# Reordering the first loads of a fused sketched-attention and GELU kernel on one Trainium2 core

## The chip, the cores and the metric

The kernel runs on one core of one Trainium2 chip. The core has five instruction streams: TensorE (PE in the profile; its weight loads are listed apart as PEld), VectorE (DVE), ScalarE (ACT), GpSimd (POOL) and SyncE (SP), which here only issues transfers. Transfers between the chip's memory and the core's on-chip buffer are issued by SyncE and, for a few, by ScalarE; sixteen DMA engines carry them out. The metric is the device time of one execution in microseconds. Before the change it is 258.27 us, the median of three runs (258.11 to 258.56).

## What is computed

Attention with polynomial sketches, for 4 batches, 4 heads, 1088 tokens and 32 channels per head, and behind it a feed-forward layer with an exact GELU:

```python
def phi(x):
    a = np.einsum('rd,bhsd->bhsr', S1, x)     # r = 8
    b = np.einsum('rd,bhsd->bhsr', S2, x)
    return np.einsum('bhsi,bhsj->bhsij', a, b).reshape(*x.shape[:-1], r * r)
q_p, k_p = phi(q), phi(k)
kv = np.einsum('bhsf,bhsd->bhfd', k_p, v)
z = np.sum(k_p, axis=2)
attn = einsum('bhsf,bhfd->bhsd', q_p, kv) / (einsum('bhsf,bhf->bhs', q_p, z)[..., None] + 1e-06)
x = attn.transpose(0, 2, 1, 3).reshape(4352, 128)
h = x @ w_in                                   # w_in: 128 x 2048
out = (0.5 * h * (1 + erf(h / sqrt(2)))) @ w_out   # w_out: 2048 x 128
```

`q`, `k` and `v` are float32. `S1`, `S2`, `w_in` and `w_out` arrive as float64; the kernel rounds them to float32 itself, with integer and float instructions on their two 32-bit words.

## The kernel before

Each batch's 1088 tokens are split into 1024 main tokens, in two chunks of 512, and a remainder of 64. The feed-forward layer runs over eight main chunks and one last chunk of all remainders. For each chunk sixteen slices of 128 hidden channels are computed (L740), put through the GELU on ScalarE (L747) and projected back (L826 and L925); between these, in a list of slots by step, the attention of the following chunks is worked out. This part begins at about 15 us and reaches to the end. Every engine's instructions keep the order of the program's text: dependencies at its end tie each instruction to the one before it on the same engine.

Ahead of it lies the start, which the change touches. It does batch 0's attention in its own way, and gets the first weights ready.

Loads. `S1` and `S2` go to one small tile, `raw_SR`. Batch 0's keys are loaded in two halves, heads 0 and 2, and heads 1 and 3 (`load_main`, L103); the queries of batch 0 in two halves by heads, each with both chunks (`load_first_q`, L120); the values by heads as the keys; the remainders' keys of batches 0 and 2 and the values of batch 0 (`load_rem`, L136). Then the first piece of `w_in` follows (`load_w_in(0)`, L181). The second piece is gated: GpSimd writes one word of its tile (L180), so that the transfer is not issued before GpSimd has come to that point. `load_rest` then issues all other weights and the other batches.

Work. TensorE first multiplies zeros into a bank that nobody reads (`keep_busy`, L957). VectorE rounds the sketches (class `Rounding`): exponent fields (L283), the scaled exponent and its clamp (L275 and L277), the low words (L278), the mantissa fields (L288), the mantissas (L302), the signs (L307), and the product, written once for each head, `SR_heads` (L317). The same class can put the low words (L270) and the clamped exponents (L294) on ScalarE, as it does for the weights. `sketches` turns `SR_heads` on TensorE (L334); VectorE makes from it `S12` (L335), the stationary sketches of the four heads, and `sT` (L337), from which GpSimd makes `Srep` (L340). `key_turn` transposes the keys of heads 0 and 2 on TensorE (L348), copied to `kT` by ScalarE (L350); `key_turn_apart` does heads 1 and 3, in two banks (L376), copied by ScalarE and VectorE (L378). `query_turn(0)` transposes chunk 0's queries on VectorE (L551). `key_features` multiplies `kT` with `S12` (L397) and forms the outer products `k_p` (L408 to L412). `expand_products` does the same for queries (L570), `expand_copy` copies (A_sb, L576), `expand_multiply` multiplies (q_pT, L581). `kv_first` sums `k_p` with the values (L445), which GpSimd and ScalarE have widened by a column of ones (L360). The remainder follows (L348, L421, L430, L451). `kz_apart` is the copied sum (L1000), `numerators_by_token` multiplies it with the queries' features (L685), `divide` divides (L696 to L700), and the turned quotient is the feed-forward layer's input `xT`. Between these VectorE, ScalarE and GpSimd round the first two pieces of `w_in` and of `w_out` (L283 to L312).

Of the kernel before, what the change touches and what calls it, by code (L numbers as in the profile page):

```python
# [16 lines left out]
def kernel(  # L17
# [18 lines left out]
    pe, dve, act, pool, sp = nc.tensor, nc.vector, nc.scalar, nc.gpsimd, nc.sync  # L36
    B, H, S, D = q.shape
    R = S1.shape[0]
# [4 lines left out]
    NP = H // 2  # L43
    J = S // 128
    MAIN = J * 128
    REM = S - MAIN
    JC = 4
# [20 lines left out]
    def work_banks():  # L68

        return wps.tile([128, 2, CW], FP, name="w_ps")  # L70

    def work_bank():
        return work_banks()[:, 0]
# [4 lines left out]
    def hidden_bank():  # L78
        return hps.tile([128, CW], FP, name="h_ps")

    def out_bank():
        return ops.tile([128, CW], FP, name="o_ps")


    by_act, by_dve, by_pool = act.copy, dve.tensor_copy, pool.tensor_copy
# [8 lines left out]
    q_first = big.tile([128, H, J, D], FP, name="q_first")  # L94
# [7 lines left out]
    def load_main(eng, n, b, heads=slice(0, H)):  # L102
        eng.dma_start(out=main[n, b][:, heads],  # L103
                      in_=src_of[n][b, heads, 0:MAIN, :].rearrange("h (p j) d -> p h j d", j=J))
# [10 lines left out]
        for g in range(4):  # L115
            sp.dma_start(out=main["v", b][g * 32:(g + 1) * 32].rearrange("t h n d -> t h (n d)"), in_=src[g])

    def load_first_q(c):
        heads = slice(2 * c, 2 * c + 2)
        sp.dma_start(out=q_first[:, heads], in_=q[0, heads, 0:MAIN, :].rearrange("h (p j) d -> p h j d", j=J))  # L120

    def load_q(n):
        at = n % NCH * CW
# [11 lines left out]
    def load_rem(n, b):  # L135
        sp.dma_start(out=rem[n][b // 2 * REM:(b // 2 + 1) * REM, b % 2],  # L136
                     in_=src_of[n][b, :, MAIN:S, :].rearrange("h p d -> p h d"))
# [13 lines left out]
    def landing(dst, wide):  # L151

        if wide:
            rows, n = dst.shape
            if n == 512:

                if not half_block:
                    half_block.append(block())
                    r = half_block[0][:, 0:2]
                else:  # L160
                    r = half_block.pop()[:, 2:4]
                raw[dst.name] = r.rearrange("p a b -> p (a b)").rearrange("p (n two) -> p n two", two=2)
            elif n == 256:
                raw[dst.name] = small(U32).rearrange("p (n two) -> p n two", two=2)
            else:
                raw[dst.name] = big.tile([rows, n, 2], U32, name=f"raw_{dst.name}")
            return raw[dst.name].rearrange("p n two -> p (n two)")
        return dst

    def words(a):  # L170

        return (a, 1) if a.dtype == FP else (a.bitcast(U32), 2)

    def load_w_in(i, gated=False):
        src, e = words(moe_w_in)
        c0, c1 = pieces[i]
        to = landing(w_in_sb[i], e == 2)
        if gated:

            pool.memset(to[0:1, 0:1], 0)  # L180
        sp.dma_start(out=to, in_=src[:, c0 * e:c1 * e])  # L181
# [10 lines left out]

    S_dst = landing(SR, S1.dtype != FP)

    for i, (queue, s) in enumerate(((act, S1), (sp, S2))):
        s, e = words(s)
        queue.dma_start(out=S_dst[i * R:(i + 1) * R, :], in_=s)
    for r, queue in enumerate((sp, act)):
        load_main(queue, "k", 0, slice(r, H, 2))
    nc.scalar.preload_act_table_set("gelu_and_others")  # L200
    for c in range(NP):
        load_first_q(c)
    load_main(sp, "v", 0, slice(0, H, 2))
    for b in (0, 2):
        load_rem("k", b)
    load_main(sp, "v", 0, slice(1, H, 2))
    load_rem("v", 0)
    load_w_in(0)

    def load_rest():  # L210
# [121 lines left out]
    def sketches():  # L332
        ps = work_bank()
        pe.transpose(ps[:, :2 * R], in_=SR_heads.rearrange("r h d -> r (h d)"), identity=ident[:2 * R, :2 * R])  # L334
        dve.tensor_mul(out=S12, in0=ps[:, None, :2 * R].broadcast_to([128, H, 2 * R]),  # L335
                       in1=mask4[:, :, None].broadcast_to([128, H, 2 * R]))
        dve.tensor_copy(out=sT, in_=ps[:, :2 * R])  # L337
        for i in range(2):
            src = sT[:, 0:R, None] if i == 0 else sT[:, None, R:2 * R]
            pool.tensor_copy(out=Srep[:, i], in_=src.broadcast_to([128, R, R]))  # L340
# [12 lines left out]
    def four_tokens(n, b, h, c):  # L353
        return main[n, b][:, h, c * JC:(c + 1) * JC, :].rearrange("p j d -> p (j d)")
# [13 lines left out]
    def key_turn(b, r, ps, copy, midway=lambda: None):  # L368
        kT[r] = transposed(ps, "kT", [four_tokens("k", b, h, c) for h in (r, r + 2) for c in range(NCH)], copy, midway)

    def key_turn_apart(b, r, banks, copies):

        kT[r] = att.tile([128, CW], FP, name="kT")
        for h, ps in zip((r, r + 2), banks):
            for c in range(NCH):
                pe.transpose(ps[:, c * 128:(c + 1) * 128], in_=four_tokens("k", b, h, c), identity=ident)  # L376
        for i, (ps, copy) in enumerate(zip(banks, copies)):
            copy(out=kT[r][:, i * 256:(i + 1) * 256], in_=ps[:, :256])  # L378
# [161 lines left out]
    def query_turn(n, copy=by_act):  # L540


        if n == 1:
            turned = transposed(hidden_bank(), "qT", [q_sb[1][:, h].rearrange("p j d -> p (j d)") for h in range(H)], copy)
            qT[n] = turned.rearrange("p (h j t) -> p h j t", h=H, j=JC)
            return
        qT[n] = att.tile([128, H, width[n] // 128, D], FP, name="qT" if n < NMAIN else "qT_rem")
        if n == 0:
            for c in range(NP):
                heads = slice(2 * c, 2 * c + 2)  # L550
                dve.transpose(out=qT[n][:, heads].rearrange("p h j t -> p h (j t)"),  # L551
                              in_=q_sb[n][:, heads].rearrange("p h j d -> p h (j d)"))
            return
        dve.transpose(out=qT[n].rearrange("p h j t -> p (h j t)"),
                      in_=q_sb[n].rearrange("p h j d -> p (h j d)") if n < NMAIN else q_rem.rearrange("p s b n d -> p (s b n d)"))
# [398 lines left out]
    def keep_busy(n, ps, cols=256):  # L954
        for i in range(n):
            noughts = [nc.const_aps.tensor(0.0, [128, m], FP) for m in (128, cols)]
            pe.matmul(ps[:, CW - cols:], lhsT=noughts[0], rhs=noughts[1], start=True, stop=True)  # L957

    bank = work_bank()
    keep_busy(2, bank, 448)  # L960
    r = Rounding(SR)
    r.fields(by_dve=True)
    r.mantissas()
    r.signs()
    r.product_for_heads(SR_heads)
    sketches()
    key_turn(0, 0, hidden_bank(), by_act)
    key_turn_apart(0, 1, [hidden_bank(), work_bank()], (by_act, by_dve))
    query_turn(0)
    widen_v(0)  # L970
    banks = [out_bank(), out_bank()]
# [185 lines left out]
    for n in range(3, NCHUNK):  # L1157

        t = (n - 1) * NF
        b = (n + 1) // 2 if n % 2 else n // 2  # L1160
# [41 lines left out]
    for t, (n, fi) in enumerate(steps):  # L1202
# [19 lines left out]
        elif fi % NB == NB - 1:  # L1222
            b = fi // NB
# [11 lines left out]
    for t in range(len(steps) + LAG):  # L1235
        if t < 4:
# [14 lines left out]
            if t == 3:  # L1251
                banks = work_banks()
# [23 lines left out]
        if t < len(steps):  # L1276
            n, fi = steps[t]
            hidden(n, fi, by_halves=t >= 18)
        if t < len(steps) and steps[t][0] < NMAIN and steps[t][1] % NB == NB - 1:
            n, b = steps[t][0], steps[t][1] // NB  # L1280
# [50 lines left out]
```

## Time and profile before

| | |
|---|---|
| median of three runs | 258.27 us |
| profiled execution | 257.91 us, of which the span from first to last instruction is 256.1 |
| stages of the span (us) | PE busy, DVE busy, ACT busy |
| 0 to 3.91 | 3.14, 1.75, 1.28 |
| 3.91 to 5.51 | 1.40, 0.42, 0.64 |
| 5.51 to 9.18 | 3.67, 3.02, 2.03 |
| 9.18 to 14.89 | 5.71, 5.42, 4.49 |
| 14.89 to 22.49 | 7.60, 6.89, 4.82 |
| 22.49 to 256.10 | 230.43, 138.51, 101.20 |

A line of the timeline gives the start in the span and the duration in us, the engine, the line of the kernel, the operation, what it writes and reads, the shapes, how often, and in brackets how long the engine was idle before it and what ended that. Times of several merged instructions run from the first one's start to the last one's end. SPq and ACTq are the streams that issue transfers; the time to landing counts from the start of the issue to the end of the transfer. The ends of matmuls are modelled, so PE counts as busy in some short waits too; the starts are the safer guide.

### The profile page before, as it was taken

To read this page: it belongs to the slowest core of one execution; us is meant where nothing else is said; L and a number is where in the kernel's file an instruction comes from. 1 tells how busy PE (TensorE), PEld (TensorE's weight loads), DVE (VectorE), ACT (ScalarE), POOL (GpSimd) and SP (SyncE) were. 2 spreads that over 40 slices of the span, in tenths; PEclk is the share of its full clock that TensorE was granted. 3 is DMA by queue.
4 is the path that set the end of the run, shared out by engine and by line. 5 is a ranking of instruction groups with operands and counts; after the bars stand their busy time and mean duration, and the time that the engine had idled before them with its cause. 6 is when DMAs were issued, how large, how long until landed. Compare 5 with 4: busy or idle time off the path is not lost.

```text
span 256.1 us, 5952 instructions
## 1 busy us (share of the span) xinstructions
PE 251.9 (98%) x2407; PEld 131.5 (51%) x2407; DVE 156.0 (61%) x330; ACT 114.5 (45%) x221; POOL 171.7 (67%) x191
## 2 busy tenths in 40 slices
PE   8999999999999999999999999999999999999994
PEld 4755444255454545454444455455544444445784
DVE  4896889969698987580278976399307000700382
ACT  3784766523535333533335332623444334433541
POOL 3413008799969777587758774787758777877950
PEclk9999999999999999999999999999999999999999
DMA  6789548610001101101000001000200200020021
GB/s 209 217 280 292 153 122 205 204 26 12 0 3 17 25 4 23 21 13 31 0 3 0 0 15 31 1 4 0 38 6 7 37 0 4 5 36 3 0 36 31
DMA packets 29083, 13.50 MB, mean 53 GB/s; under 512 B 21888, under 2 KB 27264, under 8 KB 29056
## 3 DMA queue, kind: packets, MB, share of 16 engines
q1 hardware_dynamic: 28624, 12.79, 20.1%
q8 instruction: 19, 0.31, 0.5%
q10 hardware_dynamic: 432, 0.33, 0.4%
q14 instruction: 8, 0.07, 0.1%
HBM read 10.88 MB, written 2.23 MB: 51 GB/s over the span
## 4 chain that ended last, share of the span: by engine, by line
PE 98%; ACT 0%; DVE 0%; issue 0%
PE h_ps L740 45%; PE o_ps L826 33%; PE o_ps L925 5%; PE w_ps L896 2%; PE w_ps L456 1%; PE w_ps L604 1%; PE w_ps L659 1%; PE w_ps L957 1%; PE w_ps L570 1%; PE o_ps L922 1%; PE h_ps L756 1%; PE o_ps L445 1%; PE w_ps L1043 1%; PE h_ps L348 1%; PE w_ps L685 0%; PE o_ps L397 0%
## 5 line engine op out<-in xcount | busy, mean ns | idle before, releaser
L740 PE MATMUL h_ps<-xT,w_in 128*64 128x512 f32 (+2 forms) x536 | 137.1, 568 | 0.0
L747 ACT ACTIVATE block<-h_ps 128x512 f32<-128x512 f32 (+1 forms) x128 | 73.0, 571 | 116.3 <-PE h_ps L740 114.4
L826 PE MATMUL o_ps<-block,w_out 128*64 128x256 f32 x224 | 57.5, 379 | 0.0
L740 PEld LDWEIGHTS h_ps<-xT,w_in 128*64 128x64 f32 (+1 forms) x536 | 40.7, 140 | 30.3 <-issue 11.6
L791 POOL TENSOR_TENSOR bits_low<-block 128x512 f32<-128x512 f32 x28 | 36.3, 1296 | 27.4 <-ACT block L747 27.4
L826 PEld LDWEIGHTS o_ps<-block,w_out 128*64 128x64 f32 x224 | 30.5, 137 | 38.0 <-issue 27.5
L792 POOL TENSOR_TENSOR bits_a<-block 128x512 f32<-128x512 f32 x28 | 35.7, 1276 | 11.7 <-ACT block L747 11.6
L841 DVE COPY sums<-o_ps 64x256 f32<-64x256 f32 x8 | 3.3, 417 | 60.6 <-PE o_ps L826 60.6
L793 POOL TENSOR_TENSOR bits_e<-bits_a,block 128x512 f32<-128x512 f32 x28 | 36.0, 1287 | 2.2
L794 POOL TENSOR_TENSOR bits_m<-block,bits_e 128x512 f32<-128x512 f32 x28 | 35.8, 1277 | 2.2
L826 PE MATMUL o_ps<-block,small 128*64 128x256 f32 x112 | 28.8, 379 | 0.0
L826 PE MATMUL o_ps<-bits_low,small 128*64 128x256 f32 x112 | 28.8, 379 | 0.0
L826 PE MATMUL o_ps<-bits_a,small 128*64 128x256 f32 x112 | 28.8, 379 | 0.0
L826 PE MATMUL o_ps<-bits_m,w_out 128*64 128x256 f32 x112 | 28.7, 379 | 0.0
L826 PEld LDWEIGHTS o_ps<-block,small 128*64 128x64 f32 x112 | 15.2, 137 | 17.9 <-issue 10.8
L826 PE MATMUL o_ps<-bits_e,small 128*64 128x256 f32 x112 | 17.1, 383 | 0.0
L925 PE MATMUL o_ps<-g,w_out 128*128 128x512 f32 (+1 forms) x34 | 16.5, 572 | 0.0
L826 PEld LDWEIGHTS o_ps<-bits_m,w_out 128*64 128x64 f32 x112 | 15.3, 137 | 0.0
L616 DVE STREAM_TRANSPOSE w_ps<-w_ps 128x512 f32<-128x512 f32 (+1 forms) x7 | 4.8, 687 | 17.1 <-ACT xT L670 12.7
L826 PEld LDWEIGHTS o_ps<-bits_a,small 128*64 128x64 f32 x112 | 15.2, 137 | 0.0
L826 PEld LDWEIGHTS o_ps<-bits_low,small 128*64 128x64 f32 x112 | 15.2, 137 | 0.0
L826 PEld LDWEIGHTS o_ps<-bits_e,small 128*64 128x64 f32 x112 | 7.7, 137 | 10.6 <-issue 8.8
(223 smaller groups left out, 318.5 us busy)
## 6 DMA issues: line engine op xcount, KB each, us to landing
block<-in_moe_w_in_dram SPq DMA_DIRECT2D x3, 512.0 KB, 9.8
block<-in_moe_w_out_dram SPq DMA_DIRECT2D x3, 512.0 KB, 12.0
k<-in_k_dram SPq DMA_DIRECT2D x12, 128.0 KB, 2.7
v<-in_v_dram SPq DMA_DIRECT2D x12, 128.0 KB, 3.6
q<-in_q_dram SPq DMA_DIRECT2D x24, 64.0 KB, 2.4
out_dram<-oT SPq DMA_DIRECT2D x21, 64.0 KB, 2.2
q_first<-in_q_dram SPq DMA_DIRECT2D x2, 256.0 KB, 3.8
v<-in_v_dram SPq DMA_DIRECT2D x2, 256.0 KB, 4.1
```

What stands on the lines that cost most here:

```text
L348: pe.transpose(ps[:, i * 128:(i + 1) * 128], in_=s, identity=ident)
L616: dve.transpose(out=tok, in_=ps[:, :, :H2])
L740: pe.matmul(ps[rows, :W], lhsT=w[:, rows], rhs=xT[n][:, :W], start=True, stop=True)
L747: act.activation(out=g_of[n, fi][:, :W], in_=ps[:, :W], func=ACT.Gelu)
L791: pool.tensor_sub(out=s[3], in0=a11, in1=a21)
L792: pool.tensor_add(out=s[1], in0=a21, in1=a22)
L793: pool.tensor_sub(out=s[2], in0=s[1], in1=a11)
L794: pool.tensor_sub(out=s[4], in0=a12, in1=s[2])
L826: pe.matmul(acc[n][bank][half * 64:(half + 1) * 64, col:col + HW], lhsT=fixed, rhs=moving, start=opens and e == 0 and name in "4715", stop ...
L841: dve.tensor_copy(out=N[lo, 0, one], in_=a0[lo, one])
L896: pe.matmul(acc[NMAIN][rows, COLS_REM[name]], lhsT=tokens[:, rows], rhs=fixed, start=k == 0 and name == ORDER_REM[0], stop=k == BLOCKED // ...
L925: pe.matmul(o_of[n][:, cols], lhsT=w_tile(w_out_sb, fi), rhs=g[:, cols], start=first, stop=final)
```

## The change

The issues of the first loads get another order and other queues, the sketches are rounded in part on ScalarE, their turn moves behind part of the keys' turns, and the idle multiplications get narrower.

- Both sketches are issued on ScalarE's queue, and both halves of the keys on SyncE's, as its first issues.
- The queries of batch 0 are loaded by chunks, all four heads each, not by heads. In memory a run of them is then 4 tokens of 32 channels (512 bytes) and not 8 (1 KB). Chunk 0 follows the keys; then come both halves of the values, the remainders, chunk 1, and the first piece of `w_in`.
- The two idle matmuls cover 344 columns and not 448.
- The sketches' low words and clamped exponents are made by ScalarE (L270 and L294), not VectorE (L275 to L278).
- `sketches` is called inside `key_turn_apart`, between the transposes of head 1 and of head 3.

```diff
-    def load_first_q(c):
-        heads = slice(2 * c, 2 * c + 2)
-        sp.dma_start(out=q_first[:, heads], in_=q[0, heads, 0:MAIN, :].rearrange("h (p j) d -> p h j d", j=J))
+    def load_first_q(n):
+        tokens = slice(n * JC, (n + 1) * JC)
+        sp.dma_start(out=q_first[:, :, tokens], in_=q[0, :, 0:MAIN, :].rearrange("h (p j) d -> p h j d", j=J)[:, :, tokens])
...
-    for i, (queue, s) in enumerate(((act, S1), (sp, S2))):
+    for i, s in enumerate((S1, S2)):
         s, e = words(s)
-        queue.dma_start(out=S_dst[i * R:(i + 1) * R, :], in_=s)
-    for r, queue in enumerate((sp, act)):
-        load_main(queue, "k", 0, slice(r, H, 2))
+        act.dma_start(out=S_dst[i * R:(i + 1) * R, :], in_=s)
+    for r in range(2):
+        load_main(sp, "k", 0, slice(r, H, 2))
     nc.scalar.preload_act_table_set("gelu_and_others")
-    for c in range(NP):
-        load_first_q(c)
-    load_main(sp, "v", 0, slice(0, H, 2))
+    load_first_q(0)
+    for r in range(2):
+        load_main(sp, "v", 0, slice(r, H, 2))
     for b in (0, 2):
         load_rem("k", b)
-    load_main(sp, "v", 0, slice(1, H, 2))
     load_rem("v", 0)
+    load_first_q(1)
     load_w_in(0)
...
-    def key_turn_apart(b, r, banks, copies):
+    def key_turn_apart(b, r, banks, copies, midway=lambda: None):

         kT[r] = att.tile([128, CW], FP, name="kT")
         for h, ps in zip((r, r + 2), banks):
+            if h == r + 2:
+                midway()
             for c in range(NCH):
                 pe.transpose(ps[:, c * 128:(c + 1) * 128], in_=four_tokens("k", b, h, c), identity=ident)
...
-    keep_busy(2, bank, 448)
+    keep_busy(2, bank, 344)
     r = Rounding(SR)
-    r.fields(by_dve=True)
+    r.low_words()
+    r.fields()
+    r.exponents()
     r.mantissas()
     r.signs()
     r.product_for_heads(SR_heads)
-    sketches()
     key_turn(0, 0, hidden_bank(), by_act)
-    key_turn_apart(0, 1, [hidden_bank(), work_bank()], (by_act, by_dve))
+    key_turn_apart(0, 1, [hidden_bank(), work_bank()], (by_act, by_dve), sketches)
     query_turn(0)
```

## The prediction

> **What bounds the kernel now.** I read the page first: busy shares and the chain that ended last.
>
> ```profile
> span 256.1 us, 5952 instructions
> PE 251.9 (98%) x2407; PEld 131.5 (51%) x2407; DVE 156.0 (61%) x330; ACT 114.5 (45%) x221; POOL 171.7 (67%) x191
> PE 98%; ACT 0%; DVE 0%; issue 0%
> ```
>
> TensorE is the chain, so the question is where it waits or works on nothing. The stages' busy times answer: from 22.49 to the end PE is busy 230.43 of 233.61 us, and no list of waits from there names a load that holds it up. Whatever the first 22 us gain or lose moves the rest of the program with it, one for one. So I read the start as a timeline:
>
> ```profile
> 3.14 0.86 PE L957 MATMUL w_ps<-const-float32-0.0 128*128 128x448 f32 x1
> 3.62 0.28 DVE L317 TENSOR_TENSOR SR_heads<-bits_m,bits_e 16x128 f32<-16x128 f32 x1
> 4.05 0.20 PE L334 MATMUL w_ps<-ident,SR_heads 16*128 16x16 f32 x1
> 4.18 0.66 PE L348 MATMUL h_ps<-ident,k 128*128 128x128 f32 x4
> 4.36 0.22 DVE L335 TENSOR_TENSOR S<-w_ps,mask 128x64 f32<-128x64 f32 x1 [0.46 <-PE w_ps L334]
> 4.70 0.44 PE L376 MATMUL h_ps<-ident,k 128*128 128x128 f32 x2
> 4.87 0.58 ACT L350 COPY kT<-h_ps 128x512 f32<-128x512 f32 x1 [1.77 <-PE h_ps L348]
> 5.39 0.42 DVE L378 COPY kT<-w_ps 128x256 f32<-128x256 f32 x1 [0.73 <-PE w_ps L376]
> 5.51 0.69 PE L397 MATMUL o_ps<-S,kT 128*64 128x64 f32 x16 [0.16 <-ACT kT L350]
> 5.73 0.80 DVE L551 STREAM_TRANSPOSE qT<-q_first 128x256 f32<-128x256 f32 x2
> ```
>
> The reader is to see a relay: idle columns to 4.00, the sketches' turn, the turns of the keys, ScalarE's copy, and only at 5.51 the first useful product. S12 (L335) was ready at 4.58; the copy of kT (4.87 to 5.45) came last.
>
> Then the loads, in the list of DMA issues (last column: us to landing) and VectorE's waits:
>
> ```profile
> q_first<-in_q_dram SPq DMA_DIRECT2D x2, 256.0 KB, 3.8
> k<-in_k_dram SPq DMA_DIRECT2D x1, 256.0 KB, 2.8
> k<-in_k_dram ACTq DMA_DIRECT2D x1, 256.0 KB, 3.3
> small<-in_moe_w_in_dram SPq DMA_DIRECT2D x1, 256.0 KB, 3.2
> DVE bits_e L283 <- DMA small<-in_moe_w_in_dram: 0.5, 1, 0.5
> ```
>
> With their issues (1.19 and 1.37 for the keys, 1.66 and 2.15 for the queries, 2.68 for the first values, 5.96 for the first w_in) they land at 3.97, 4.67, 5.36, 6.05, 6.78 and 9.16. 256 KB every 0.70 us: a full pipe, in which w_in is last, and VectorE waits 0.53 us for it. From 9.18 to 14 VectorE is busy 95% (5.42 of 5.71 us to 14.89), and it feeds what PE waits for there. So two arms matter: keys to products (PE, ScalarE), and the arrival of w_in (VectorE).
>
> **The change, part by part.**
>
> *Loads.* The first keys' issue moves from 1.19 to SyncE's first place, 0.73. They landed 2.78 us after issue: 3.51. The rest follows at the pipe's pace: second keys 4.21 (4.67 before). They leave ScalarE's queue and the second sketch takes their place there, so both issues of that queue still end at 1.79, and its table load still runs 1.82 to 3.10. SyncE loses one issue (0.40) and gains one (0.42).
> The queries now come as runs of 512 bytes, 512 of them per load, not 256 of 1 KB. The trace has 256 runs of 1 KB at 0.70, and 256 of 128 bytes (each remainder) at 0.28: from first values (6.78) to remainder values (8.32) are 1.54, less 0.70 for the second values, over three. Linear in runs and bytes this gives 0.92 for the new form; the low end is 0.70, as before. I take 0.80, between them, since the runs lie nearer to 1 KB than to 128 bytes in what they carry. [...]
> So chunk 0's queries land at 5.01, values at 5.71 and 6.41, three remainders at 7.25, chunk 1's queries at 8.05, w_in 0.84 later (its step before) at 8.89, against 9.16: 0.27 earlier, between 0.03 (0.92 each) and 0.47 (0.70 each). SyncE is not the limit: five issues of 0.42 to 0.49 and three of 0.60 to 0.76 bring w_in's issue to 5.9 as before, and an issue on an empty pipe (the second w_in, 8.5) took 2.8.
> Chunk 1's queries, moved past both values and three remainders, are read at 10.12 by L348: 2 us of cover. Values and remainders only come earlier. GpSimd's widening of v waits for values (6.83 before) and starts at 5.7, then waits for ScalarE's a_t; its memset that gates the second w_in moves from 8.42 to about 7.7. That buys nothing: that w_in, landed by 11.3, is first read at 12.08.
>
> *Sketches.* The second one is issued at 1.37 and not 0.73; the pair landed 1.57 after issue, so 2.94, at worst with the first keys whose packets it shares the engines with, 3.51. I take 3.05, nearer the small load. VectorE loses three instructions (0.17, 0.17, 0.16). ScalarE gains two; the nearest row is a_rem, 128x64, 0.21. They lie in its 1.77 us of idleness. The first can't start before the table load ends at 3.10. Chain: e 0.39 (3.44), r on ScalarE 0.21 plus handover (3.75), signs to SR_heads 0.48 as before (3.42 to 3.90): 4.23, 0.33 later than now.
>
> *PE's order.* Idle columns: four records, 0.75 from start to start, scaled by 344/448 to 0.58: they end at 3.26 and not 4.00. The keys' turns then wait for the landing at 3.51, start at 3.55 and end 0.66 later, 4.21. ScalarE copies from 4.24 to 4.82. Behind them two turns for head 1 (landed 4.21; 4.25 to 4.53), the sketches' turn at 4.53 (SR_heads has been there for 0.3), S12 from 4.84 to 5.06, and first products at 5.12 against 5.51: 0.39 gained. Two turns of head 3 and its copy sit behind the sketches' turn on PE: head 3 turned by 5.0, VectorE's copy after S12 and sT, at 5.12 against 5.39, second products 5.6 against 6.03. VectorE then runs its packed row (qT, k_p) 0.27 earlier, and chunk 0's queries (5.01) are there in time for qT at 5.46.
>
> *Sum.* The PE and ScalarE arm gains 0.39 up to A_sb and kz_apart (8.86 and 10.24 now); the VectorE arm gains 0.27 at w_in, where it would otherwise wait. The smaller one decides, since both meet at the numerators' division (11.49): 0.27 us. The profiled execution took 257.91 (256.1 of span and 1.81 around it), 0.36 below the median of three, 258.27; the sum gives 257.64 on its scale, **258.00** on the median's.
>
> **Rivals.**
>
> *PE is still slow when the keys come (slower).* The loads of the weights show two speeds of the array: 335 ns for 128 columns among the idle columns, 138 ns in the keys' turns.
>
> ```profile
> L957 PEld LDWEIGHTS w_ps<-const-float32-0.0 x4: 285/335/337, 0.7 to 2.4; 128*128 128x128 f32 x4
> L348 PEld LDWEIGHTS h_ps<-ident,k x4: 138/140/142, 4.2 to 4.5; 128*128 128x128 f32 x4
> ```
>
> The switch lay after 2.4 and before 4.02, with PE at work since 0.77. Now the columns end at 3.26 and PE pauses a quarter of a microsecond; turns that begin at 3.55 may still run slowly, 0.2 us more each. Three slow ones eat the gain (copy of kT to 5.42). With all up to the sketches' turn slow (3.55 plus six by 0.335 is 5.56, 0.51 for the turn itself, 0.28 for S12) products start at 6.35, 0.84 late: 259.1. With the 32 products slow too (16 loads take 0.55, so 34 ns more each, 1.1 us) 260.2. It decides if the speed comes later than about 4.5, and costs over 0.52 from about 5.5.
> For it: idle columns exist only to fill this time. Against it: the switch in the trace may lie well before 3.5; the last idle record is 0.10 shorter than the middle ones (857 to 954 ns).
> [...]
>
> *Nothing is gained.* The queries' 512-byte runs cost 0.92 each, w_in lands at 9.13, and all that PE wins is spent waiting there: 258.2.
>
> *More is gained.* Full rate for the queries, w_in at 8.69, and VectorE's first instruction on it, which took 0.64 after the wait (0.28 to 0.41 elsewhere), finds data nearly there. With PE's arm at its 0.39 and this 0.2 more: 257.6 to 257.75.
>
> **How the numbers follow.** 0.2% is 0.52 us, about what a measurement of this kernel tells from no change. Forecast (gain of 0.1 to 0.55): 0.46, of which 0.06 lies beyond 0.52. More gained: 0.14, at its far end beyond it too. Nothing gained: 0.13. Slow PE: 0.27, all slower. Faster 0.20, same 0.53, slower 0.27. The forecast's own range is 257.75 to 258.2; 257.5 to 259.1 takes in both gains and the nearer half of the slow case, leaving out some 0.17.
>
> **What would show it.** Right: first keys' turn near 3.55 with loads at 138 ns, first products near 5.1, w_in landing near 8.9, VectorE still waiting for it a few tenths, and the stage from 22 us on unchanged in length and shifted by 0.3. Wrong: loads of 280 ns or more behind 3.5; SR_heads after 4.5, with PE idle before L334; queries landing over 0.9 after the keys; or a new wait of the division (11.49) on something not named here.

## The result, and the profile after

The changed kernel takes 259.02 us in the median (22 executions, 258.22 to 260.15), the kernel before beside it 258.28 (22 executions, 257.94 to 258.81): a ratio of 1.0033, 95% interval 1.0019 to 1.0046. It is slower by about 0.85 us by the ratio, and by 0.74 between the medians, where 0.27 us of gain was forecast.

The two ranges say as much as the medians. Sorted, the changed kernel's times fall into two groups: twelve from 258.22 to 259.10, none in between, ten from 259.61 to 260.15. The kernel before has one group only. Even the first group's median, 258.67, lies 0.4 above that of the kernel before. The profile was taken of an execution of the first group (258.30, span 256.5), so it shows only one part of the story; a profile of the second group comes with the experiments.

First the page of the changed kernel (span, busy shares, chain by engine), which has changed little:

```profile
span 256.5 us, 5953 instructions
PE 252.2 (98%) x2407; PEld 132.2 (52%) x2407; DVE 155.7 (61%) x327; ACT 115.1 (45%) x223; POOL 172.2 (67%) x191
PE 97%; DMA 1%; ACT 0%; DVE 0%; issue 0%
```

Then its timeline (start, duration, engine, line, what, and in brackets the idle time before it and what ended that); lines behind the insertion of the diff have moved by two, so L399 is the old L397:

```profile
0.77 2.63 PE L959 MATMUL w_ps<-const-float32-0.0 128*128 128x344 f32 x4 [0.77 <-PEq L1318]
3.55 0.71 PEld L348 LDWEIGHTS h_ps<-ident,k 128*128 128x128 f32 x4 [1.16 <-POOL v_rem_aug L245]
3.64 0.17 DVE L283 TENSOR_SCALAR bits_e<-raw_SR 16x32 uint32<-16x32 uint32 x1 [2.54 <-DMA raw_SR<-in_S_dram]
4.25 0.43 PEld L378 LDWEIGHTS h_ps<-ident,k 128*128 128x128 f32 x2
4.47 0.28 DVE L317 TENSOR_TENSOR SR_heads<-bits_m,bits_e 16x128 f32<-16x128 f32 x1
4.71 0.58 ACT L350 COPY kT<-h_ps 128x512 f32<-128x512 f32 x1 [0.48 <-PE h_ps L348]
4.86 0.14 PEld L334 LDWEIGHTS w_ps<-ident,SR_heads 16*128 16x128 f32 x1 [0.17 <-DVE SR_heads L317]
5.20 0.23 DVE L335 TENSOR_TENSOR S<-w_ps,mask 128x64 f32<-128x64 f32 x1 [0.45 <-PE w_ps L334]
5.54 0.58 PEld L399 LDWEIGHTS o_ps<-S,kT 128*64 128x64 f32 x16 [0.32 <-ACT kT L350]
6.04 0.77 DVE L553 STREAM_TRANSPOSE qT<-q_first 128x256 f32<-128x256 f32 x2
9.29 0.29 DVE L283 TENSOR_SCALAR bits_e<-small 128x256 uint32<-128x256 uint32 x1 [0.41 <-DMA small<-in_moe_w_in_dram]
```

The keys do come earlier, and their turns start at 3.55 and not 4.18. But the four weight loads of the first turns take 0.71 us, not 0.42, and the two of head 1 take 0.43, not 0.20: the array is at its lower rate until between 4.46 and 4.86. The slow turns start 0.21 us apart (3.82, 4.03, 4.25, 4.46), those of the kernel before 0.11 (4.35, 4.46, 4.56): about half the rate. The sketches are read at 3.64 and not 2.30; the PE waits 0.17 us for `SR_heads`. The first products start at 5.54, where they started at 5.51 before. The head start of 0.63 us is used up within 2 us, even in this quick execution. The first `w_in` (issued at 6.14, 3.1 to landing) is read at 9.29, 0.11 later than before.

### The profile page after: what moved, and what is told of

Read it like the earlier page. It is cut to its first block, busy times and chain, and to the rows that moved or that the text cites. A ratio compares the mean times of both kernels' runs of the same rounds, so it can differ in the third digit from the quotient of the medians.

```text
span 256.5 us, 5953 instructions
## 1 busy us (share of the span) xinstructions
PE 252.2 (98%) x2407; PEld 132.2 (52%) x2407; DVE 155.7 (61%) x327; ACT 115.1 (45%) x223; POOL 172.2 (67%) x191
## 4 chain that ended last, share of the span: by engine, by line
PE 97%; DMA 1%; ACT 0%; DVE 0%; issue 0%
PE h_ps L742 45%; PE o_ps L828 33%; PE o_ps L927 5%; PE w_ps L898 2%; PE w_ps L458 1%; PE w_ps L606 1%; PE w_ps L661 1%; DMA k<-in_k_dram 1%; PE w_ps L572 1%; PE o_ps L924 1%; PE h_ps L348 1%; PE h_ps L758 1%; PE o_ps L447 1%; PE w_ps L1046 1%; PE w_ps L687 0%; PE o_ps L399 0%
## 5 line engine op out<-in xcount | busy, mean ns | idle before, releaser
L742 PE MATMUL h_ps<-xT,w_in 128*64 128x512 f32 (+2 forms) x536 | 137.1, 568 | 0.0
L742 PEld LDWEIGHTS h_ps<-xT,w_in 128*64 128x64 f32 (+1 forms) x536 | 40.7, 140 | 30.3 <-issue 11.6
```

Source lines behind the costliest of these rows:

```text
L742: pe.matmul(ps[rows, :W], lhsT=w[:, rows], rhs=xT[n][:, :W], start=True, stop=True)
```

## The experiments

Two reasons compete for the loss, with a third that the forecast had leant on. *Clock theory*: the narrower idle columns leave the PE without work before the keys have landed, and the array then gets its full rate late. *Sketch theory*: the second sketch, behind the keys' issue, delays `S12`. *Load theory*: the queries' 512-byte runs and the new order delay the queries and `w_in`. Each set of runs had executions of the kernel before beside it on the same chip. In the table "late" counts executions at 259.6 us and above.

| kernel | median us (lowest to highest) | late | ratio to before, 95% interval |
|---|---|---|---|
| before, in four sets | 258.36, 258.50, 258.41, 258.63 (257.92 to 258.93) | 0 of 34, 35, 29, 17 | |
| changed, again | 259.34 (258.16 to 261.93) | 6 of 12 | 1.0040 [1.0015, 1.0066] |
| changed, 448 columns | 258.65 (258.16 to 260.86) | 1 of 12 | 1.0012 [0.9994, 1.0030] |
| changed, 512 columns | 259.05 (258.22 to 260.98) | 1 of 12 | 1.0025 [1.0008, 1.0042] |
| changed, second sketch on SyncE first | 259.91 (258.56 to 261.08) | 7 of 12 | 1.0053 [1.0034, 1.0073] |
| changed, the same and 448 columns | 258.66 (258.45 to 259.28) | 0 of 11 | 1.0010 [1.0001, 1.0019] |
| before, 344 columns | 259.47 (258.94 to 260.35) | 5 of 11 | 1.0047 [1.0032, 1.0061] |
| before, 400 columns | 258.59 (257.99 to 260.45) | 5 of 12 | 1.0030 [1.0006, 1.0054] |
| before, 512 columns | 258.62 (257.97 to 259.06) | 0 of 12 | 1.0000 [0.9991, 1.0010] |
| before, a pause among the columns | 259.24 (258.16 to 260.21) | 4 of 12 | 1.0024 [1.0008, 1.0041] |
| before, sketches rounded in part by ScalarE | 258.42 (258.06 to 258.80) | 0 of 11 | 1.0001 [0.9992, 1.0009] |
| before, the new order behind the keys | 258.43 (258.09 to 258.81) | 0 of 11 | 1.0000 [0.9991, 1.0009] |
| before, chunk 1's queries behind w_in | 258.57 (257.88 to 258.78) | 0 of 12 | 1.0001 [0.9991, 1.0011] |

### The idle columns, undone and done alone

```diff
-    keep_busy(2, bank, 344)      # in the changed kernel
+    keep_busy(2, bank, 448)
```

> The changed kernel with 448 idle columns again, nothing else undone. Clock theory (the array is at half rate when the keys are turned, and gets its full rate at a time that varies from run to run): with PE kept at work to about 4.0 the keys' loads take 138 ns in every run, the spread of the changed kernel (258.2 to 260.2) shrinks to under 1 us, and the median falls to 258.0 to 258.5, about 0.5 to 1 us under the changed kernel. Sketch theory (the second sketch lands behind the keys, SR_heads at 4.75 and not 3.90): nothing in the idle columns touches that; the median stays within 0.2 us of 259.0 and first products start at 5.5 to 5.6. Load theory (512-byte runs of the queries, w_in at 9.24): the same as the sketch theory, 259.0.

```diff
-    keep_busy(2, bank, 448)      # in the kernel before
+    keep_busy(2, bank, 344)
```

> The kernel before with 344 idle columns, the only edit. Clock theory: PE runs out of idle columns at 3.4 and waits until 4.05 for the sketches, so the keys are turned at half rate in part of the runs: spread over 1 us, median 258.8 to 259.8. Sketch theory and load theory: no load and no rounding has moved, the sketches' turn still waits for SR_heads at 3.90; 258.3 within 0.2, spread as before.

Measured: 258.65 with the columns restored, all but one execution (260.86) at 258.92 or less; 259.47 with only the columns narrowed in the kernel before, five of eleven late, and the other six (258.94 to 259.47) also above every execution of the kernel before (258.93 at most). This one number in the kernel before costs as much as the whole change (1.0047 against 1.0033 and 1.0040, with intervals that overlap). The sketch theory and the load theory expected 259.0 and 258.3 and missed on both sides. The clock theory's figures came in for the narrowed columns. For the restored ones it came nearest, but 258.65 is above its 258.0 to 258.5, one execution broke its spread, and its 138 ns for the keys' loads was wrong. In the profile with 448 columns restored they were still slow (line, count, then least, middle and most nanoseconds, then first and last start):

```profile
L348 PEld LDWEIGHTS h_ps<-ident,k x4: 181/226/226, 3.4 to 4.3; 128*128 128x128 f32 x4
```

Full rate came there between 4.32 and 5.00, in time for the products.

The profile of the narrowed kernel before is of a late execution (260.29). The loads of one weight tile in its products, first of the kernel before:

```profile
L397 PEld LDWEIGHTS o_ps<-S,kT x16: 132/138/138, 5.5 to 5.9; 128*64 128x64 f32 x16
```

and of the kernel before with 344 columns:

```profile
L397 PEld LDWEIGHTS o_ps<-S,kT x16: 182/227/231, 6.1 to 6.8; 128*64 128x64 f32 x16
```

138 ns against 227 ns for the same loads, and the sixteen start over 0.7 us and not 0.4. This goes on to the expanded products: there the last slow load starts at 8.99, and the first at 138 ns is the remainder's turn at 9.97.

### The changed kernel once more

> The changed kernel once more, for a second profile and five more times. Clock theory: times spread from 258.2 to 260.2 again; where the profiled run is one of the long ones, its extra time over 258.3 lies before 15 us, as weight loads of 220 ns and more that go on after 4.5. Sketch theory: the times' spread has another place in the trace, or none that the start shows.

Six of twelve were late again, among them the profiled one (259.91, span 258.1). Its timeline of weight loads:

```profile
6.04 0.94 PEld L399 LDWEIGHTS o_ps<-S,kT 128*64 128x64 f32 x16 [0.33 <-ACT kT L380]
6.85 0.98 PEld L399 LDWEIGHTS h_ps<-S,kT 128*64 128x64 f32 x16
7.95 0.33 PEld L572 LDWEIGHTS w_ps<-qT,Srep 32*64 32x64 f32 x16
9.68 0.14 PEld L348 LDWEIGHTS h_ps<-ident,k_rem 128*128 128x128 f32 x1 [0.55 <-issue]
```

Here the same kernel does its first sixteen loads in 0.94 us, which took 0.58 in the quick execution, and the remainder's turn comes at 9.68, which came at 7.91 there: 1.77 us later. The spans differ by 1.6 us (258.1 and 256.5). So the late group's time is lost before 9.7 us, in which the array runs at its lower rate.

Read across all fourteen profiles, a later full rate goes with a longer span. The second column gives the starts of the last slow load (160 ns or more) and of the first one at full rate. The third is where the trace's own record of the granted clock, at full clock, begins; it lies between the two in every profile, within 0.03 us. (The views print a clock of 1.00 for the time ahead of this record too.)

| profile | last slow, first full load (us) | record of full clock from | span us |
|---|---|---|---|
| before | 2.40, 4.02 | 3.77 | 256.1 |
| before, 512 columns | 2.62, 4.26 | 4.01 | 256.4 |
| before, a pause among the columns | 3.73, 4.28 | 4.09 | 256.4 |
| before, the new order behind the keys | 4.30, 4.49 | 4.46 | 256.3 |
| changed | 4.46, 4.86 | 4.62 | 256.5 |
| before, sketches rounded in part by ScalarE | 4.67, 4.82 | 4.75 | 256.5 |
| changed, 448 columns | 4.32, 5.00 | 4.94 | 256.7 |
| before, 400 columns | 5.14, 5.31 | 5.25 | 256.6 |
| changed, 512 columns | 5.40, 5.75 | 5.49 | 257.1 |
| changed, 448 columns, second sketch first | 5.77, 6.23 | 5.89 | 257.3 |
| before, chunk 1's queries behind w_in | 6.64, 6.72 | 6.68 | 257.0 |
| changed, second sketch first | 8.71, 9.07 | 9.03 | 258.1 |
| changed, again | 8.91, 9.68 | 9.41 | 258.1 |
| before, 344 columns | 8.99, 9.97 | 10.00 | 258.4 |

The order has a few exchanges among neighbours, 257.3 ahead of 257.0 the largest. From the first weight load of the feed-forward layer (L740, in the changed kernel L742) to the end all fourteen take 241.5 us within 0.02: every difference of the spans arises ahead of it. One kernel's switch moves from execution to execution, 4.62 and 9.41 in the changed one; and two profiles whose idle work has 448 columns and runs without a pause into the first turns have it at 3.77 and at 6.68.

### How much idle work is enough

```diff
-    keep_busy(2, bank, 448)      # in the kernel before
+    keep_busy(2, bank, 400)
```

> The kernel before with 400 idle columns: PE's idle work ends near 3.75, a third of the way back from 448 to 344 still missing, and the sketches' turn starts at 4.03 as before. Clock theory with a threshold in how long PE must have worked: some of the executions at 259.6 and above (none of 448's, about half of 344's), median 258.4 to 259.2. If any pause of 0.15 us or more is enough, about half of the executions lie there, as with 344. If the idle columns only had to fill the time, no change: 258.4, none above 259.3.

```diff
-    keep_busy(2, bank, 448)      # in the kernel before
+    keep_busy(2, bank, 512)
```

> The kernel before with 512 idle columns, the only edit. PE is at them until 4.45, so the keys are turned 0.4 us later. Clock theory: full rate by then in every run, so only that delay shows: median 258.5 to 258.8, spread under 0.8 us, none over 259.3. If instead only the length of the columns counts and the rate does not, the same change of 0.4 with the opposite sign should have come from 344 columns, which cost 1.1 us.

With 400 columns seven executions are at 257.99 to 258.69 and five at 260.22 to 260.45; nothing lies between. This shortage of idle work does not make every execution a little slower; it makes a part of them, here five of twelve, slower by 2 us. (With 344 columns the others were slower too.) The profile, of a quick execution (258.49), shows the pause that all of them have: columns to 3.77, then 0.27 us in which PE waits for the sketches' turn:

```profile
0.77 3.00 PE L957 MATMUL w_ps<-const-float32-0.0 128*128 128x400 f32 x4 [0.77 <-PEq L1315]
4.05 0.25 PE L334 MATMUL w_ps<-ident,SR_heads 16*128 16x16 f32 x1 [0.27 <-DVE SR_heads L317]
```

More columns cost nothing in the kernel before: 512 of them end with the sketches' turn at 4.26, 0.2 later, products at 5.76, and yet the ratio is 1.0000. The median, 258.62, is within the 258.5 to 258.8 that I expected, but the kernel before beside it had 258.50, so the delay of 0.4 us that I meant to see in it is not there. That a surer full rate pays for the later start is an argument here, not a measurement.

### A pause, with the end of the idle work kept

```diff
-    keep_busy(2, bank, 448)      # in the kernel before
+    keep_busy(1, bank, 448)
+    noughts = nc.const_aps.tensor(0.0, [128, 128], FP)
+    pe.matmul(bank[:, CW - 256:], lhsT=noughts, rhs=v_rem_aug[0].rearrange("p h d -> p (h d)"), start=True, stop=True)
+    keep_busy(1, bank, 160)
```

> The kernel before with its idle work cut in three: 448 columns, then 256 that read the tile v_rem_aug, which GpSimd has filled only at 2.66, then 160. PE pauses from 2.4 to about 2.7 and is then at work until 4.1 as before. [...] If what counts is that PE is at work up to the moment when the keys land (or the number of idle columns, here 432 for each idle matmul on average), there is none above 259.3 and the median is 258.41 within 0.2.

```profile
0.77 1.83 PE L957 MATMUL w_ps<-const-float32-0.0 128*128 128x448 f32 x2 [0.77 <-PEq L1318]
2.72 1.22 PE L962 MATMUL w_ps<-v_rem_aug,const-float32-0.0 128*128 128x256 f32 x2
3.73 0.62 PE L957 MATMUL w_ps<-const-float32-0.0 128*128 128x160 f32 x2
4.28 0.13 PEld L334 LDWEIGHTS w_ps<-ident,SR_heads 16*128 16x128 f32 x1 [0.21 <-issue]
```

Work goes on to 4.28, longer than before, and there is only a gap near 2.5 (the ends of matmuls are modelled, so the timeline does not show its full width). Five executions are at 258.16 to 258.37, seven at 259.23 to 260.21, four of them late. So it is not enough that PE is at work when the keys land: a short pause on the way makes a part of the executions slower. That it does so by putting the full rate off is inferred from the other profiles; this one is of a quick execution (258.27), with full rate by 4.28.

### The sketches' queue

```diff
-    for i, s in enumerate((S1, S2)):      # in the changed kernel
+    for i, (queue, s) in enumerate(((act, S1), (sp, S2))):
         s, e = words(s)
-        act.dma_start(out=S_dst[i * R:(i + 1) * R, :], in_=s)
+        queue.dma_start(out=S_dst[i * R:(i + 1) * R, :], in_=s)
```

> The changed kernel with the second sketch ahead of the keys on SyncE's queue again; the keys then follow on that queue. Sketch theory: the pair lands near 2.3, SR_heads is there near 3.9 (ScalarE's table load ends at 3.0), the sketches' turn no longer holds up the turns of head 3, S12 comes near 5.0 and the time falls by 0.3 to 0.5 us to about 258.5. Clock theory: the keys land 0.45 later, at 4.0, with PE idle from 3.4 on, so the rate is no better; median 259 or above, and a spread over 1 us again.

The same, with 448 columns:

> The changed kernel with 448 idle columns and with the second sketch on SyncE's queue ahead of the keys. Sketch theory, for what is left of the loss once the columns are back (258.65 against 258.36): SR_heads comes near 3.65 and no longer at 4.5, the products start at 5.5 or before, and the median is 258.0 to 258.4. If the loads' order behind the keys is what remains, nothing moves: 258.5 to 258.8. Clock theory: the spread stays under 1 us but for single runs, keys' loads at 138 ns.

`SR_heads` came at 3.64 in both, more than 1 us earlier than in the changed kernel (4.75), and nothing was gained: 259.91 with 344 columns, 258.66 with 448, against 259.34 and 258.65 with the sketches late. The profile with 448 columns:

```profile
3.36 0.28 DVE L317 TENSOR_TENSOR SR_heads<-bits_m,bits_e 16x128 f32<-16x128 f32 x1
4.03 0.71 PEld L348 LDWEIGHTS h_ps<-ident,k 128*128 128x128 f32 x4 [1.29 <-issue]
```

The keys' turns now start at 3.97 and 4.03, with the array still slow, and the sketches' turn stands behind six of them, at 5.4 and 5.5. So `S12` did not come earlier but later, at 6.07 and 6.12 against 5.43 and 5.82 in the two profiles of the changed kernel, and the two runs do not test what an earlier `S12` is worth. They show that the early sketches alone are worth nothing in this order; that the sketches are not the main cause rests on the runs with the columns. Seven late of twelve with 344 columns, none of eleven with 448, is again the columns' doing.

### Rounding on ScalarE alone, the new order of loads alone

```diff
-    r.fields(by_dve=True)      # in the kernel before
+    r.low_words()
+    r.fields()
+    r.exponents()
```

> The kernel before with the sketches' low words and clamped exponents on ScalarE, nothing else. SR_heads at 3.6 to 3.7 and not 3.90, but PE is at idle columns until 4.0: 258.36 within 0.2 us by every theory that puts the loss elsewhere. If putting the rounding on ScalarE costs something (its copy of kT, its table load), it is over 258.6.

```diff
+    load_first_q(0)      # in the kernel before, with load_first_q by chunks
+    for r in range(2):
+        load_main(sp, "v", 0, slice(r, H, 2))
+    for b in (0, 2):
+        load_rem("k", b)
+    load_rem("v", 0)
+    load_first_q(1)
     load_w_in(0)
```

> The kernel before with the queries by chunks and the changed kernel's order of loads behind the keys (chunk 0, values, remainders, chunk 1, w_in); sketches, keys and columns as before. Load theory: chunk 0 lands after 5.6 and holds up its transposes, and w_in lands at 9.2 to 9.4: median 258.6 to 259. Clock theory and sketch theory: 258.36 within 0.2.

1.0001 and 1.0000: neither does anything by itself. ScalarE's rounding did not bring `SR_heads` forward, to the 3.6 to 3.7 that I expected, but back: 4.07 against 3.90. With the order alone `w_in` was read at 9.17 after a wait of 0.45, as before (9.18, 0.53). The load theory is out as a cause of the loss, and with it my fear for the 512-byte runs, and my hope that the order alone would bring `w_in` sooner.

### w_in ahead of chunk 1's queries

```diff
     load_rem("v", 0)      # in the run above (kernel before, new order)
-    load_first_q(1)
     load_w_in(0)
+    load_first_q(1)
```

> The kernel before with the queries by chunks and chunk 1 behind w_in, so that w_in lands about 0.7 us earlier than in the kernel before, near 8.5. Two-arms theory (VectorE's arm and the arm of PE and ScalarE meet at the division, the later one decides): VectorE no longer waits for w_in but then for PE's numerators: 258.4 within 0.2. If w_in alone held up the start, 0.4 to 0.5 us are gained: 257.9 to 258.0.

VectorE's wait for the first `w_in` is gone, and another has taken its place:

```profile
9.05 0.40 DVE L366 COPY v_rem_aug<-v_rem 64x128 f32<-64x128 f32 x1
9.37 0.28 DVE L283 TENSOR_SCALAR bits_e<-small 128x256 uint32<-128x256 uint32 x1
10.34 1.28 DVE L581 TENSOR_TENSOR q_pT<-A_sb,w_ps 128x512 f32<-128x512 f32 x2 [0.50 <-ACT A_sb L576]
12.32 0.17 DVE L696 TENSOR_SCALAR den_tok<-h_ps 128x8 f32<-128x8 f32 x1 [0.36 <-PE h_ps L685]
```

It now waits 0.50 for ScalarE's copy and 0.36 for PE's numerators. The ratio is 1.0001 [0.9991, 1.0011]: a `w_in` that is there in time gains at most some 0.2 us alone. That the arm of PE and ScalarE then sets the end is shown for this execution only. Its array is slow until 6.68, and its products begin 0.63 later than in the profile of the kernel before:

```profile
6.14 0.77 PEld L397 LDWEIGHTS o_ps<-S,kT 128*64 128x64 f32 x16 [0.33 <-ACT kT L350]
```

In the quick profile of the changed kernel VectorE does not wait for the numerators (L698 there, at 11.82).

### The changed kernel with still more columns

```diff
-    keep_busy(2, bank, 344)      # in the changed kernel
+    keep_busy(2, bank, 512)
```

> The changed kernel with 512 idle columns: PE is at work without a pause until about 4.3, when both halves of the keys have landed. Clock theory: none above 259.6, spread under 1 us, median 258.3 to 258.7, what is left above the kernel before being the later sketches. If the rest of the change has a cost of its own that 448 columns hid in part, the median is 258.8 or more without a wide spread.

One late execution of twelve, so the second group is gone; but the rest lie at 258.22 to 259.33, the median of all is 259.05, and my 258.3 to 258.7 was missed. In its profile PE waits once more between the keys' turns, because the second half of the keys lands late:

```profile
4.32 1.06 PE L348 MATMUL h_ps<-ident,k 128*128 128x128 f32 x4
5.33 0.25 PEld L378 LDWEIGHTS h_ps<-ident,k 128*128 128x128 f32 x2 [0.36 <-DMA k<-in_k_dram]
5.75 0.13 PEld L334 LDWEIGHTS w_ps<-ident,SR_heads 16*128 16x128 f32 x1 [0.17 <-issue]
```

Issued at 1.2, it was read at 5.33 here, at 5.00 with 448 columns, at 4.59 in the second profile of the changed kernel, and at 4.25 in the first; with a queue for each half it was read at 4.70 in the kernel before, and at 5.01, after a wait, in that with 512 columns. Behind the loads there was no reserve: the sketches' turn, and with it `S12`, stand behind head 1.

No version beat the kernel before. The edits that left it equal gained nothing, and every version with both halves of the keys on one queue has a median above it, by 0.16 us at the least; with 448 columns alone (1.0012) the interval takes in no change.

## Why the prediction was wrong

*Idle columns: the step that failed.* I priced narrower columns as a gain, idle work that ends at 3.26 and not 4.00, and kept the slow array as a rival with 0.27. Done alone in the kernel before, the narrower columns cost 1.1 us (259.47 against 258.36). The argument against the rival was that the switch "may lie well before 3.5". It does not: no profile shows a full-rate load before 4.02, where one was done between 3.5 and 4.0 it was slow, and in the kernel before the record of full clock begins at 3.77. And with a pause of a quarter of a microsecond, which I had written down, 16 of 34 executions of the changed kernel were late; the profiled one of these has the switch at 9.4. The rival was right in what it named (the loads of the first keys' turns took 179 to 230 ns in the changed kernel, and not 138), in its place, and in "it decides if the speed comes later than about 4.5". That the median (259.02) lies so near the 259.1 that it gave is in part chance: it falls between the two groups.

*Its size.* I took 0.2 us for each slow load from the idle columns' 335 ns. Among the keys' turns the slow load is 227 ns against 138, 0.09 each. The four turns of the first bank lost 0.29 (0.71 against 0.42), where I had 0.8. My sign of this rival, loads of 280 ns or more, could not have shown them. For the products I had doubled the 0.55 us of sixteen loads; in the late profile they took 0.94. The case with slow products behind them, 260.2, was about right as a sum (the late group is at 259.6 to 260.15), by luck in its parts: in the late profile the products begin 0.53 late, not 0.84, and the slow expanded products, which it left out, make up for it.

*What sets the moment of the switch.* This the runs leave open. They show two groups of times with one program (258.22 to 259.10 and 259.61 to 260.15), a full rate that comes at 3.77 in one profile and at 6.68 in another with no pause before the first turns, and at 9.03 to 10.00 in the late ones with one, and late executions wherever the pause is, near 2.5 (4 of 12), 3.5 (16 of 34) or 3.9 (5 of 12), too few to tell the shares apart.

*Keys.* Landed at 3.51 by forecast, first turn at 3.55 by forecast and measurement: right. The second half at 4.21, read at 4.25: right in this profile, 0.3 to 1.1 late in three others with the same loads. The forecast took the pipe's pace from two queues at work and carried it over to one. Why one queue's second load is at times so late was not settled.

*Sketches.* I took 3.05 for their landing, with 3.51 as the worst: VectorE read them at 3.64, 3.86, 3.42 and 3.33 in four profiles. `SR_heads` came at 4.75 and not 4.23. In the quick execution this cost PE's arm its 0.39 of gain: `S12` was ready at 5.43, not 5.06, and the first products follow it at 5.54, where 5.12 was forecast. What it costs the median was not measured; the runs with the columns leave little room for it.

*Loads.* Chunk 0's queries landed at 6.0 (1.75 and 4.3 to landing), forecast 5.01; `w_in` at 9.27, forecast 8.89, with its issue 0.2 later than I took it. The 0.80 us for the new form was not too low in itself: in five of the eight profiles that have it, the queries landed 0.7 to 0.8 behind the second keys, about the 0.70 of 256 KB in runs of 1 KB. In the other three it was 1.3 to 1.9, and why is open. By itself the form cost nothing (1.0000).

*The sum.* Neither gain that it compares was there: in the quick profile PE's arm gained nothing (its first products at 5.54 against 5.51), and `w_in` was read 0.11 later. That the smaller one decides was not shown. An earlier `w_in` alone gained nothing, and there VectorE waited for A_sb and for the numerators instead, but in an execution whose PE was slow until 6.68.

*What stays open.* With the columns at 448 the changed kernel is at 1.0012 [0.9994, 1.0030], with the sketch moved as well at 1.0010 [1.0001, 1.0019]. With 512 it is at 1.0025 [1.0008, 1.0042]. Some 0.1 to 0.2% may be left to the rest of the change. The order behind the keys and the rounding, each alone in the kernel before, are out as its cause; the keys on one queue, the second sketch behind them and the place of the sketches' turn were not tried each by itself. Nor is it shown why one execution of twelve was late with 448 and with 512 columns in the changed kernel; PE waits there for the second keys, at 4.5 to 5.0 and 5.0 to 5.3 in the profiles.

## What to carry to other kernels

The idle work ahead of the first products was part of the schedule here: when loads come earlier, do not cut it to the new landing, but leave it overlapping the first real work, since more of it cost nothing in the kernel before (512 columns for 448: 1.0000), and with less five of twelve executions (400 columns) and five of eleven (344) were late, by up to 2 us. Look at the spread before the median: the two groups with an empty stretch between them (259.10 to 259.61) were here a switch at 4.6 in one profile and at 9.4 in the other, and one profile shows only one side. And a wait that a profile shows on an engine (0.53 us for `w_in`) need not be a gain: taken away alone it was worth nothing (1.0001). Try that before building on it.

## What the runs showed of the hardware

- The array has two rates at the start, seen in the same weight load at 138 ns (kernel before, L397) and 227 ns (with 344 columns), and in the keys' turns, which start 0.11 us apart in the kernel before and 0.21 in the changed one. In the five profiles of the kernel before and its variants with PE at work from 0.77 to the first turns (but for a wait of 0.1 us in one), full rate came between 3.8 and 6.7; in the six with a pause of some 0.15 to 0.6 us ahead of them, between 4.1 and 10.0.
- In the changed kernel a load of 2 KB issued on ScalarE's queue at 1.38, while 512 KB were under way on SyncE's, was read 2.26 us after its issue (3.64); with nothing ahead of it, in the kernel before, 1.57 (issued at 0.73, read at 2.30).
- Two loads of 256 KB one behind the other on a single queue landed 0.7 us apart in the first profile of the changed kernel, and 1.0, 1.7 and 2.0 us apart in three others with the same loads (its second one, with 448 columns, with 512).
